# Loading one half of a weight tile in eight small transfers, one behind each of the next eight weight transfers

## The chip, the cores and the metric

The kernel runs on one core of a Trainium2 chip. The metric is device time in microseconds (us) of a whole execution; the profile gives the span of the same execution, which is some 1.7 us shorter. The kernel before takes 437.2 us; its trace comes from a slower execution, of 438.8 us (span 437.0).

## The reference, cut to what matters

```python
def reference(q, k, v, f, w_r, w_i, w_ch):         # names shortened
    # q, k, v: (8, 8, 576, 64); attention with a decay from f, causal
    x = attention(q, k, v, f)                      # ... (8, 576, 512)
    X = np.fft.rfft(x, axis=1)[:, :64]             # 64 modes
    Yr = einsum('bmd,mde->bme', Xr, w_r) - einsum('bmd,mde->bme', Xi, w_i)
    Yi = einsum('bmd,mde->bme', Xr, w_i) + einsum('bmd,mde->bme', Xi, w_r)
    y = np.fft.irfft(Y, n=576, axis=1)
    u = x + y
    return u + np.maximum(u @ w_ch, 0.0)
```

`w_r` and `w_i` have 64 x 512 x 512 fp32 elements each, 134 MB together. Reading them sets the pace: 163.73 MB are read from HBM in 437 us.

## The kernel before

The weights come in 64 tiles. Each tile has a `w_r` and a `w_i` transfer, issued by Pool (GpSimd), which also casts fp32 to bf16. A transfer reads 1 MiB. Tiles go through a ring of nine buffers; attention runs on TensorE meanwhile, and the matmuls of a tile (`emit_modes`) are put between attention steps.

```python
NRING = 9
wpool = ctx.enter_context(tc.tile_pool(name="wpool", bufs=NRING))
keep = tc.keep_in_program_order

def pool_dma(dst, src):
    keep(nc.gpsimd.dma_start(dst, src))

def emit_w_load(n):
    dc, g = tile_of(n)
    if n < NTH:                                  # the first 32 tiles
        wb = wb_tile(n, MG, 2 * D)
        for t, src in enumerate((moe_w_r, moe_w_i)):
            pool_dma(
                wb[t:128:2, :, :],               # 64 partitions
                src[g * MG : (g + 1) * MG, dc * 128 : (dc + 1) * 128, :]
                .rearrange("m (p r) e -> p m (r e)", r=2),
            )
    else:                                        # the last 32: 128 partitions each
        wb = wb_tile(n, 2, M2, 2 * D)
        ...
                pool_dma(wb[:, t, ms, :], src[...]...)
    wtiles[n] = wb

# ... in the attention loop, step s:
    if s > B:
        while nmode < (s - B) * NTH // (NS - B):
            emit_modes(nmode)                    # matmuls of one tile
            nmode += 1
            next_w()                             # load of the next one
```

The softmax here doesn't subtract the row's maximum and nothing guards it: scores larger than these inputs give would overflow.

## Time and profile before

| | before |
|---|---|
| time, median of 3 timed runs | 437.21 us (436.98 to 437.32) |
| span in the trace | 437.0 us |
| transfers from Pool until the last weights | 178, over 8 semaphores in turn |
| last weights landed | 400.66 us |
| start of the last eight weight matmuls | 401.18 us |
| spread of the 16 engines at that landing | 8.03 us |

### The profile page before, as it was taken

The numbers are of one execution on the slowest core, as the hardware profiler recorded it, in microseconds if no ns is written. First come the engines' busy times: TensorE is split into PE (matmuls) and PEld (weight loads), VectorE is DVE, ScalarE is ACT, GpSimd is POOL, SyncE is SP. The second block draws the span as 40 slices with busy tenths as digits, with TensorE's granted clock in tenths as the row PEclk, the third lists the DMA queues.
The fourth block names the chain that finished last, engine by engine and source line by source line (L and its number), as shares of the span: only waits on it lengthen the run. The fifth ranks groups of instructions, "written<-read, shape, count | busy, mean of one in ns | idle before, by whom it ended". The sixth has DMA issues, their size and how long they took to land.

```text
span 437.0 us, 12197 instructions
## 1 busy us (share of the span) xinstructions
PE 359.5 (82%) x5247; PEld 245.5 (56%) x5265; DVE 263.3 (60%) x658; ACT 224.6 (51%) x340; POOL 128.9 (29%) x202
## 2 busy tenths in 40 slices
PE   3787799998897887978778796999999688998880
PEld 2454666676666665656556664666665354554440
DVE  5797778877565655655657677333334353753891
ACT  2887478775534537446355473234335242742780
POOL 7333332233233233232332231323232223200600
PEclk9996699998866858556668688699999898998997
DMA  8999999999999999999999999999999999993797
GB/s 185 233 235 244 230 236 238 237 214 234 233 215 236 228 220 237 211 237 233 215 237 211 211 212 211 211 211 211 211 211 212 211 211 211 211 207 73 253 366 270
DMA packets 50981, 97.37 MB, mean 223 GB/s; under 512 B 3792, under 2 KB 12976, under 8 KB 50928
## 3 DMA queue, kind: packets, MB, share of 16 engines
q0 software_dynamic: 46688, 86.16, 100.6%
q1 hardware_dynamic: 3920, 9.91, 6.3%
q8 instruction: 41, 0.67, 0.6%
q10 hardware_dynamic: 320, 0.52, 0.5%
q14 instruction: 12, 0.10, 0.1%
HBM read 163.73 MB, written 9.44 MB: 396 GB/s over the span
## 4 chain that ended last, share of the span: by engine, by line
PE 31%; DMA 29%; ACT 12%; DVE 11%; issue 4%; ACTq 0%; DVEq 0%; POOL 0%
DMA wb<-in_moe_w_i_dram 27%; ACT E L574 8%; PE pav L612 7%; PE ps L567 6%; PE A L188 5%; PE tp L305 5%; DMA stv<-in_v_dram 3%; DVE QTs L320 2%; PE px L655 2%; PE vp L539 2%; ACT KT L318 2%; PE pz L826 2%; PE pu L826 1%; DVE os L1004 1%; DVE XT L669 1%
## 5 line engine op out<-in xcount | busy, mean ns | idle before, releaser
L574 ACT ACTIVATE E<-ps 128x1024 bf16<-128x1024 f32 (+1 forms) x128 | 101.5, 853 | 22.8 <-PE ps L567 12.7
L188 PE MATMUL A<-XT,wb 128*128 128x16 bf16 x1984 | 70.3, 181 | 14.6 <-DMA wb<-in_moe_w_i_dram 9.6
L188 PEld LDWEIGHTS <-wb 128*128 128x128 bf16 x1984 | 63.5, 99 | 28.6 <-issue 11.9
L93 POOL DMA_DIRECT2D wb<-in_moe_w_r_dram x64 | 42.5, 664 | 120.7 <-DMA wb<-in_moe_w_r_dram 24.5
L567 PE MATMUL ps<-QTs,KT 64*128 64x64 bf16 (+4 forms) x384 | 57.6, 320 | 18.2 <-ACT E L574 16.3
L93 POOL DMA_DIRECT2D wb<-in_moe_w_i_dram x64 | 42.4, 663 | 86.6 <-DMA wb<-in_moe_w_i_dram 42.9
L612 PE MATMUL pav<-va,E 128*128 128x65 bf16 (+1 forms) x1088 | 55.5, 210 | 3.1 <-DVE x_all L634 2.6
L612 PEld LDWEIGHTS <-E 128*128 128x128 bf16 (+1 forms) x1088 | 45.5, 115 | 17.5 <-issue 8.1
L589 DVE TENSOR_TENSOR E<-E,trimask 128x256 bf16<-128x256 bf16 (+2 forms) x128 | 36.9, 303 | 20.2 <-ACT E L574 20.0
L324 ACT COPY VT<-tp 128x640 bf16<-128x640 bf16 (+1 forms) x32 | 23.2, 762 | 33.5 <-PE tp L305 33.5
L865 ACT CAST XW<-pxw 128x512 bf16<-128x512 f32 x36 | 20.7, 586 | 35.8 <-PE pxw L858 23.5
L567 PEld LDWEIGHTS <-KT 64*128 64x128 bf16 x384 | 19.2, 99 | 32.8 <-issue 21.1
L908 ACT CAST XW<-pB 128x512 bf16<-128x512 f32 x36 | 20.9, 586 | 31.4 <-PE pB L826 25.8
L318 ACT COPY KT<-tp 128x640 bf16<-128x640 bf16 (+1 forms) x32 | 22.0, 751 | 26.2 <-PE tp L305 26.0
L907 DVE CAST x_all<-pA 128x512 bf16<-128x512 f32 x36 | 24.9, 692 | 16.7 <-PE pA L826 15.2
L858 PE MATMUL pxw<-wch,yy 128*128 128x512 bf16 x133 | 33.7, 386 | 1.2 <-issue 0.7
L320 DVE COPY QTs<-tp 128x640 bf16<-128x640 bf16 (+1 forms) x32 | 23.3, 767 | 14.2 <-PE tp L305 14.0
L634 DVE TENSOR_TENSOR x_all<-pav,rcp 128x384 bf16<-128x384 f32 x64 | 29.2, 456 | 0.9
L153 DVE TENSOR_TENSOR YTe<-A,Yacc 128x128 bf16<-128x128 f32 x16 | 5.9, 368 | 33.2 <-PE A L188 33.2
L623 DVE RECIPROCAL rcp<-pav 128x6 f32<-128x6 f32 x64 | 12.1, 190 | 22.6 <-PE pav L612 21.8
L826 PEld LDWEIGHTS <-ident_bf 64*64 64x64 bf16 (+1 forms) x300 | 14.5, 110 | 17.0 <-issue 9.6
L539 PE MATMUL vp<-ident_bf,VT 128*128 128x128 bf16 x160 | 17.2, 249 | 4.8 <-DVE QTs L320 4.3
(143 smaller groups left out, 609.8 us busy)
## 6 DMA issues: line engine op xcount, KB each, us to landing
wb<-in_moe_w_r_dram POOLq DMA_DIRECT2D x62, 512.0 KB, 17.2
wb<-in_moe_w_i_dram POOLq DMA_DIRECT2D x62, 512.0 KB, 17.8
stv<-in_v_dram POOLq DMA_DIRECT2D x10, 576.0 KB, 15.4
out_dram<-os SPq DMA_DIRECT2D x10, 512.0 KB, 6.3
stk<-in_k_dram POOLq DMA_DIRECT2D x11, 288.0 KB, 15.4
stq<-in_q_dram POOLq DMA_DIRECT2D x11, 288.0 KB, 15.2
wx<-in_v_dram POOLq DMA_DIRECT2D x5, 576.0 KB, 15.1
out_dram<-uo SPq DMA_DIRECT2D x3, 512.0 KB, 3.6
```

What stands on the lines that cost most here:

```text
L93: keep(nc.gpsimd.dma_start(dst, src))
L188: nc.tensor.matmul(A[:, eb, mi, :], lhsT=w_of(mi, eb * 128), rhs=x_of(m), start=(i == 0), stop=(i == len(terms) - 1),)
L318: nc.scalar.copy(rows(KTs[pr % 2][:, :, 0:S]), tv)
L320: ins = nc.vector.tensor_copy(rows(QT[pr][:, :, :]), tv)
L539: nc.tensor.transpose(vp[:, sc, :, :].rearrange("p b d -> p (b d)"), VTs[s // 2 % 2][:, h, sc * 128 : (sc + 1) * 128], ident_bf[:, :],)
L567: nc.tensor.matmul(ps[:, b, o : o + n], lhsT=KTs[pr % 2][bs, h, jb * 128 : (jb + 1) * 128], rhs=QT[pr][bs, h, jb * 128 + c0 : jb * 128 + c ...
L574: nc.scalar.activation(E[:, :, piece * 512 : piece * 512 + w], ps[:, :, 0:w], ACT.Exp, scale=scale,)
L589: nc.vector.tensor_tensor(dg, dg, tr, ALU.mult)
L612: nc.tensor.matmul(pav[64 * half : 64 * half + w, slot, :], lhsT=E[:, b, c : c + (w - 1) * st + 1 : st], rhs=va[:, jb, b, :], start=(n == ...
L634: nc.vector.tensor_tensor(xo, pi, ri, ALU.mult)
L826: return nc.tensor.matmul(p, lhsT=lhsT, rhs=rhs, start=first, stop=not first, skip_group_check=True)
L858: nc.tensor.matmul(pxw[:, :], lhsT=xT[:, eb, i * 128 : (i + 1) * 128], rhs=wch[:, eb, :], start=(eb == 0), stop=(eb == NDC - 1),)
```

## The change

It is meant to move work from one half of the 16 transfer engines to the other. The `w_r` part of tile 17 (index 16) is not loaded in one transfer on all engines, but in eight transfers of eight partitions, one behind each of the next eight weight transfers; a tiny transfer of eight partitions goes ahead of each, and only moves the place at which the next small one starts.

```diff
+    UPPER = 16
+    tiny = const.tile([8, 8, MG, 4], BF16, name="tiny")
+    eighths = []
+
-    def pool_dma(dst, src):
+    def pool_dma(dst, src, more=False):
         keep(nc.gpsimd.dma_start(dst, src))
+        for pair in eighths[:1] if more else ():
+            for d, s in pair:
+                keep(nc.gpsimd.dma_start(d, s))
+            eighths.pop(0)
...
             for t, src in enumerate((moe_w_r, moe_w_i)):
+                if n == UPPER and t == 0:
+                    for j in range(8):
+                        rows = src[
+                            g * MG : (g + 1) * MG, dc * 128 + 16 * j :, :
+                        ][:, 0:16, :].rearrange("m (p r) e -> p m (r e)", r=2)
+                        big = wb[16 * j : 16 * j + 15 : 2, :, :], rows
+                        small = tiny[:, j, :, :], rows[:, :, 0:4]
+                        eighths.append((small, big))
+                    continue
                 pool_dma(
...
+                    True,
                 )
```

More of the change, by code (lines that the diff above doesn't have):

```diff
@@ L132, in emit_modes @@
         wb = wtiles.pop(n)
+        assert n != UPPER or not eighths
         nm = MG if n < NTH else M2
```

## The prediction

> **What bounds the kernel now.** I read the page's slices first, then its queue part, then who waited for whom on the Pool engine, then the chain of waits, then the last part of the timeline.
>
> ```profile
> DMA  8999999999999999999999999999999999993797
> ...
> q0 software_dynamic: 46688, 86.16, 100.6%
> ...
> q8 instruction: 41, 0.67, 0.6%
> ...
> q14 instruction: 12, 0.10, 0.1%
> HBM read 163.73 MB, written 9.44 MB: 396 GB/s over the span
> ```
>
> The transfer engines are busy in every slice until the weights are in; nearly all of it is the Pool queue (q0). Two small queues fetch instructions: 41 blocks of 16,384 bytes on q8, and q14. They look like nothing (0.6% and 0.1%), but that is a mean over 16 engines.
>
> ```profile
> POOL wb L93 <- DMA wb<-in_moe_w_r_dram: 55.2, 31, 2.5
> POOL wb L93 <- DMA wb<-in_moe_w_i_dram: 55.2, 33, 2.7
> ```
>
> Pool itself spends its time waiting for earlier weight transfers: the built program gives its transfers eight semaphores in turn, so one is issued when the eighth before it has landed on all its engines. Eight are in flight.
>
> ```profile
> 276.12 18.28 DMA wb<-in_moe_w_i_dram
> 294.40 0.29 issue
> 294.69 19.60 DMA wb<-in_moe_w_i_dram
> 314.28 0.29 issue
> 314.57 19.60 DMA wb<-in_moe_w_i_dram
> ```
>
> From 276 to 395 us the chain is transfer after transfer, each issued 0.29 us after the landing that freed its semaphore.
>
> ```profile
> 393.50 0.21 PE L188 MATMUL A<-XT,wb 128*128 128x16 bf16 x2
> ...
> 395.07 0.91 PE L188 MATMUL A<-XT,wb 128*128 128x16 bf16 x30 [1.36 <-DMA wb<-in_moe_w_i_dram]
> ...
> 401.18 0.36 PE L172 MATMUL A<-XT,wb 128*128 128x16 bf16 x8
> ```
>
> TensorE waits 1.36 us for the weights of the last tile but one, and starts the last eight of the last tile at 401.18, 0.52 us after its last piece landed (400.66 in the trace). So the end of the kernel, some 36 us later, hangs on the *last* landing of the last weights, and could follow it forward by about 1.4 us before TensorE itself is the bound.
>
> **The view that the change is about** is not on the page. Each Pool transfer leaves 16 semaphore increments in the trace, one per transfer engine. In order of time, relative to the last of the 16, in us:
>
> ```
> landing at   7.5 us: -1.07 to -0.85 (nine), -0.64 to -0.45 (five), -0.35, 0
> landing at 395.0 us: -7.44 -7.40 -7.29 -7.22 -6.89 -6.67 -6.30 | -4.30 | -3.03 -2.95 -1.40 -1.21 -1.17 -0.76 -0.73 0
> ```
>
> A transfer has landed when the slowest engine is done, and that engine is 7.4 us behind the fastest when the last weights come. The increments carry no engine's name, so I followed each lane from transfer to transfer (a lane keeps its place to 0.1 us until it jumps). Eight lanes jump by about 1.2 us four or five times each, and end 7.27, 6.56, 6.45, 6.31, 6.18, 5.99, 4.43 and 4.37 us behind the three fastest. Eight never make that jump: seven end between -0.04 and 1.09, one creeps to 3.05 in steps of 0.4 to 0.6. The times of the q8 blocks (39 before 400 us) match the jumps, and the blocks' durations repeat with period eight (974, 974, 961, 892, 893, 949, 945, 936 ns): TensorE's instructions are fetched by eight of the sixteen engines in turn. The creeping lane fits q14's blocks of 322 ns.
>
> **What the Trainium skill says.**
> - "Runtime: NRT & Kernel Launch", section "Instruction fetch mechanics": instructions are refilled in 16 KiB blocks by the sequencer's own transfer queue. The trace agrees (41 of 16,384 bytes). The page calls the cost mostly hidden; here one block holds its engine back about 1.2 us.
> - "DMA: Bandwidth & Descriptors", "Why a DMA increments its semaphore by 16 and not by 1": from Pool all 16 engines post an increment whatever the shape; a transfer of k < 16 runs on k consecutive engines from a round-robin cursor. The kernel before shows the 16 increments; it has no transfer of fewer than 16 partitions from Pool, so the cursor is shown by nothing here.
> - The same page, "Specifications": about 27 GiB/s per engine. Here a weight transfer of 1 MiB read takes 2.485 us on an undisturbed lane: 65,536 bytes per engine, 26.4 GB/s. Agrees roughly; the engines run at their limit.
> - The same page, "Rules for kernel authors": below 64 KB a transfer is mostly overhead. The kernel before has none in its busy stage.
>
> **The change part by part.** It takes tile 17's w_r transfer away (64 partitions, all engines alike), and brings the same bytes in eight transfers of 8 partitions. With k = 8 each uses eight engines; the tiny one (8 partitions too) moves the cursor by eight first, so that all eight big ones fall on the same half and the tiny ones on the other. The intent must be to take work from the half that fetches instructions. In the built program the eighths stand behind the transfers of w_i of tile 17 to w_r of tile 21 (issued between 119 and 147 us now); TensorE needs tile 17 only nine tiles later.
>
> Per engine, a = cost of one extra transfer in the queue:
> - Half relieved: -2.485 us, plus 16 a, plus the tiny pieces (32 of 16 bytes per engine).
> - Half loaded: -2.485 + 8 x 16,384 bytes / 27.36 GB/s (the slope between 36,864 bytes in 1.437 and 65,536 in 2.485) = +2.31 us, plus 16 a.
> - a: that line leaves 1.437 - 1.347 = 0.09 us at zero bytes; yet w_ch has twice the descriptors of a weight transfer in 2.44 us, so it may be nearer 0. I take 0.05: 16 a = 0.8 us. Tiny pieces: 0.5 us (a guess).
>
> If the relieved half is the fetching one, its slowest lane goes from 7.27 to 7.27 - 2.485 + 0.8 + 0.5 = 6.1; the loaded half's slowest goes from 3.05 to 3.05 + 2.31 + 0.8 = 6.2. The last landing comes 7.27 - 6.2 = 1.1 us earlier. Of the 1.36 us that TensorE waits there, this fits: the end moves by 1.1 us. 437.2 - 1.1 = **436.1 us**.
>
> Beside other work: 15 more Pool issues of about 0.5 us (14 issues of 16 KB take some 0.5 us each now) while Pool idles most of the time. No compute is touched.
>
> **The rivals.**
> 1. *The big ones land on the fetching half, or on four of it.* For it: nothing in the trace names the half, and the cursor could start elsewhere. Against: the tiny transfers make no sense unless someone knew the half. Then 7.27 becomes 7.27 + 2.31 + 0.8 = 10.4: the end is 3.1 us later, 440.3 us. The same comes out if a transfer of 8 partitions always takes the same engines and these fetch.
> 2. *The ring of eight runs dry.* Tiny and small transfers take semaphores, so that when w_i of tile 19 is issued only two full transfers (4.95 us) lie ahead on the relieved half; less 0.3 for the wait and about 1.3 for two issues, 3.3 us. Against: at 82.0 us in the kernel before, an issue ended with 2.97 us ahead on the fastest lane and no gap followed. A gap would cost a few tenths at most, and mainly on the fast lanes, which have time.
> 3. *Nothing moves.* If a is 0.09, 16 a is 1.44 and the gain shrinks to 0.4 us; if the tiny pieces cost 0.2 us each on an engine, to about 0. That is 436.8 to 437.2 us. With a = 0.02 it is 1.6 us, and TensorE's 1.36 us of slack caps it: about 435.8.
>
> **Range and chances.** I give the intended half 0.72, with 435.4 to 437.2 us, middle 436.1; the wrong or mixed half 0.28, with 439 to 441. The middle of both together is a little over 436.1: **436.3 us**; 8 in 10 from **435.2** to **440.2**, wide on the slow side for rival 1. Two per cent is 8.7 us; no branch reaches it: faster 0.005, within 0.985, slower 0.01.
>
> **What would show it.** Right: before the last weights the spread of the 16 increments falls from 7.4 to about 5 to 6 us, with the two groups merged instead of seven and nine apart; TensorE's wait of 1.36 us before the last tile but one shrinks or moves earlier with the landing; the chain from 276 us stays transfer after transfer; the engines' share stays at 9 in every slice. From 165 to about 220 us the loaded half should lag, so landings come about 1 to 1.5 us *later* than before. Wrong: the spread grows to about 10 us (rival 1); Pool's transfers around 120 to 165 us are issued late with a dip in the transfer slices (rival 2); the spread falls as told but every lane is late by the same amount (rival 3).

## More of the kernel before

The order of Pool's transfers is pinned (`keep`); the order of the matmuls among the attention work is not: the scheduler chooses it when the kernel is built, from when it expects data.

The columns are 40 equal slices of the span (10.9 us each); PEclk is the granted TensorE clock in tenths, GB/s what the transfer engines moved:

```profile
PEclk9996699998866858556668688699999898998997
GB/s 185 233 235 244 230 236 238 237 214 234 233 215 236 228 220 237 211 237 233 215 237 211 211 212 211 211 211 211 211 211 212 211 211 211 211 207 73 253 366 270
```

The transfer engines move 207 GB/s or more in every slice after the first until the weights are in. The clock drops to half in the attention part and, for one slice or so, late.

## The result, and the profile after

The changed kernel takes 440.93 us (440.61 to 441.39, 4 runs) beside 437.23 us (436.98 to 437.32): ratio 1.0086, 95% interval 1.0069 to 1.0104. A ratio is the mean time of one kernel's runs over that of the other's of the same rounds, so not quite the ratio of the medians. The change makes the kernel 3.7 us slower; predicted were 436.3 us and a range up to 440.2. A second set on another chip gave 441.21 us and 1.0090. All outputs are right.

The page of the changed kernel (slices of 11.0 us):

```profile
DMA  8999999999999999999999999999999999994797
GB/s 181 234 235 244 232 235 238 236 218 230 235 211 231 197 203 224 220 238 226 222 235 212 211 210 212 210 211 212 211 212 210 212 210 211 211 211 88 251 362 271
...
q0 software_dynamic: 47696, 86.16, 100.5%
...
q8 instruction: 41, 0.67, 0.6%
```

The digits of the DMA row hide it, the GB/s row shows it: in the 14th and 15th slice, 143 to 165 us, the engines moved 197 and 203 GB/s, where they moved 228 and 220 before. That is where the small transfers are. The bytes are the same; q0 has 1008 packets more.

Who Pool waited for, in us, times, longest:

```profile
POOL wb L97 <- DMA wb<-in_moe_w_i_dram: 44.6, 28, 2.2
POOL wb L97 <- DMA wb<-in_moe_w_r_dram: 33.1, 18, 2.3
POOL wb L97 <- PE A L207: 32.8, 10, 7.7
```

The waits for earlier transfers fell from 110.4 to 77.7 us, and the wait for TensorE's weight matmuls is 32.8 us, where the first trace before has

```profile
POOL wb L93 <- PE A L188: 13.2, 5, 5.7
```

This sum shows nothing by itself: in the second trace of the kernel before (below) it is 30.9 us, with a longest of 7.7 us. What is new is one place, the issue of `w_r` of tile 26, nine tiles behind tile 17. Before and after:

```profile
180.09 0.63 POOL L93 DMA_DIRECT2D wb<-in_moe_w_r_dram  x1 [1.71 <-PE tp L305]
188.70 0.63 POOL L97 DMA_DIRECT2D wb<-in_moe_w_r_dram  x1 [7.04 <-PE A L207]
```

The semaphore of this transfer had been free for 0.5 us in both traces of the kernel before, and for 5.8 us here. There TensorE frees a ring buffer later than before, which the prediction excluded.

The chain of waits is as before, transfer after transfer with 0.29 us between:

```profile
289.09 18.14 DMA wb<-in_moe_w_i_dram
307.23 0.29 issue
307.52 19.59 DMA wb<-in_moe_w_i_dram
327.12 0.29 issue
327.41 20.28 DMA wb<-in_moe_w_i_dram
```

TensorE at the end:

```profile
398.01 0.91 PE L207 MATMUL A<-XT,wb 128*128 128x16 bf16 x30 [0.92 <-DMA wb<-in_moe_w_i_dram]
...
403.43 0.36 PE L191 MATMUL A<-XT,wb 128*128 128x16 bf16 x8 [0.39 <-DMA wb<-in_moe_w_i_dram]
```

The last eight matmuls start at 403.43 us, 2.25 us later than before, again behind the last landing (403.39). The end follows the landing: 439.5 - 403.39 = 36.1 us, before 437.0 - 400.66 = 36.3 us.

Now the 16 increments, which no view prints; they are taken from the trace's semaphore records. The first fence has their times relative to the last at the landing of the last weights, the second the step of the lanes from the tiny transfer to the eighth behind it. A lane is one of the 16 engines as the increments show it, without a name. A step is the difference of the n-th landings, the earliest first; where one lane overtakes another, the two mix.

```
last weights, before         -8.03 -8.03 -7.90 -7.85 -7.51 -7.30 -6.35 -4.74 -3.21 -3.11 -1.53 -1.23 -1.19 -1.07 -0.90 0
last weights, after          -7.07 -7.04 -6.84 -6.60 -6.56 -6.53 -6.16 -5.43 -4.13 -3.39 -0.92 -0.77 -0.75 -0.33 -0.25 0
last weights, after (second) -5.64 -5.61 -5.50 -5.42 -5.29 -5.03 -4.75 -4.25 -2.53 -2.48 -1.83 -1.43 -0.18 -0.16 -0.13 0
```

```
after,          1st eighth (135.6 us)  0.20 0.46 0.19 0.19 0.22 0.28 0.35 0.20 | 0.20 0.21 0.56 0.55 0.54 0.50 0.67 0.73
after (second), 8th eighth (165.5 us)  0.18 0.18 0.18 0.19 0.18 0.20 0.20 0.20 | 0.48 0.42 0.72 0.72 0.56 0.63 0.64 0.74
```

A lane that carries an eighth takes 0.42 to 0.75 us, one that does not 0.18 to 0.2; the values between them are such mixtures. The eighths went to the **late** lanes, those that also fetch TensorE's instructions. This is the prediction's first rival.

### The profile page after: what moved, and what is told of

The parts are those of the page before. It is cut to its first block, busy times and chain, and to the rows that moved or that the text cites. A ratio compares the mean times of both kernels' runs of the same rounds, so it can differ in the third digit from the quotient of the medians.

```text
span 439.5 us, 12212 instructions
## 1 busy us (share of the span) xinstructions
PE 359.4 (82%) x5247; PEld 245.8 (56%) x5265; DVE 263.8 (60%) x658; ACT 225.0 (51%) x340; POOL 137.4 (31%) x217
## 4 chain that ended last, share of the span: by engine, by line
PE 36%; DMA 26%; DVE 11%; ACT 10%; issue 4%; POOL 1%; ACTq 0%; DVEq 0%
DMA wb<-in_moe_w_i_dram 25%; PE pav L631 8%; ACT E L593 7%; PE A L207 6%; PE ps L586 6%; PE tp L324 6%; PE px L674 2%; PE vp L558 2%; DVE QTs L339 2%; ACT KT L337 2%; DVE os L1023 1%; DVE XT L688 1%; DVE E L608 1%; PE px L699 1%; PE pz L845 1%
## 5 line engine op out<-in xcount | busy, mean ns | idle before, releaser
L97 POOL DMA_DIRECT2D wb<-in_moe_w_r_dram x63 | 42.3, 672 | 124.5 <-PE A L207 32.8
L586 PE MATMUL ps<-QTs,KT 64*128 64x64 bf16 (+4 forms) x384 | 58.5, 327 | 17.6 <-ACT E L593 15.6
L97 POOL DMA_DIRECT2D wb<-in_moe_w_i_dram x64 | 42.5, 663 | 67.6 <-DMA wb<-in_moe_w_i_dram 36.1
L642 DVE RECIPROCAL rcp<-pav 128x6 f32<-128x6 f32 x64 | 12.1, 190 | 23.1 <-PE pav L631 22.4
```

Of the source, the lines that this page charges most:

```text
L586: nc.tensor.matmul(ps[:, b, o : o + n], lhsT=KTs[pr % 2][bs, h, jb * 128 : (jb + 1) * 128], rhs=QT[pr][bs, h, jb * 128 + c0 : jb * 128 + c ...
```

## The experiments

There were eighteen runs, three of them repeats, each on one chip with the kernel before beside it. "Mean" and "slowest" below are how much longer the lanes took than in the kernel before from the landing of `w_i` of tile 16 to that of `w_i` of tile 22 (the window of the small transfers), the mean over the 16 lanes and the last lane. "The ring" is from here on that of the eight semaphores, and it is "dry" when a lane has too little work left in it to stay busy.

### Tiny one behind

```diff
-                        eighths.append((small, big))
+                        eighths.append((big, small))
```

> Each tiny transfer stands behind its eighth instead of ahead of it; bytes, counts and places in the queue are the same, so if a cursor deals out halves, tiny and big ones change halves. Theory A (eighths fell on the fetching half, and every one of the 16 small transfers costs about 0.18 us on all 16 engines): the fetching lanes get -2.485 + 16 x 0.18 = +0.4 us, the other half carries the data, the end is at about 437.6 us (437.0 to 438.4). Theory B (the half plays no part, only the number of small transfers and the ring of eight): as the changed kernel, 440.5 to 441.3 us.

> The changed kernel with the tiny transfer behind (as in the first experiment) once more, on another chip: if the half explains part of the 3.7 us, it is faster than the changed kernel beside it by 1 to 3 us; last weights landing 2 to 3 us earlier than there. If the half explains nothing, within 0.5 us of it.

Measured: 440.02 us (438.14 to 442.81), ratio 1.0069 (1.0036 to 1.0101), and on the other chip 440.61 us, 1.0076 (1.0061 to 1.0092), where the changed kernel beside it took 441.21. The steps of the lanes turned round: in the first trace the first eighth took 0.61 to 0.74 us on lanes among the nine earliest and 0.16 to 0.17 on the latest.

```
tiny behind, 1st eighth (134.5 us)  0.33 0.41 0.28 0.61 0.62 0.63 0.73 0.65 0.74 | 0.16 0.17 0.37 0.45 0.19 0.17 0.17
tiny behind, 8th eighth (164.8 us)  0.17 0.17 0.16 0.18 0.17 0.16 0.18 0.20 | 0.64 0.65 0.67 0.62 0.63 0.66 0.66 0.68
```

So the order of the pair decides the half, and the prediction's intended half needs the tiny one *behind*. But by the eighth eighth the loaded lanes are themselves the latest eight. In the first trace the last weights landed at 400.34 us, 3.1 us before the changed kernel's, and the profiled span was 436.4 us; TensorE waited as before:

```profile
395.20 0.91 PE L207 MATMUL A<-XT,wb 128*128 128x16 bf16 x30 [0.98 <-DMA wb<-in_moe_w_i_dram]
...
400.39 0.36 PE L191 MATMUL A<-XT,wb 128*128 128x16 bf16 x8 [0.19 <-DMA wb<-in_moe_w_i_dram]
```

In the second trace they landed at 403.30, as late as the changed kernel's. (The first trace is of the fastest of that kernel's six executions, 438.14 us.) One trace of this kernel is therefore not enough to tell its landing; the times are. They say: right half 2.8 to 3.3 us slower than the kernel before, and only some 0.6 us faster than the wrong half on the same chip. Both theories of the first expectation missed the 440.02 us. The second asked for 1 to 3 us and a landing 2 to 3 us earlier, and missed both. Something common to both orders costs more than the half does.

### No tiny one

```diff
-                        eighths.append((small, big))
+                        eighths.append((big,))
```

> The eight eighths without the tiny ones: eight small transfers instead of sixteen, and halves that alternate. Theory A: -2.485 + 8 x 0.18 + 4 eighths of about 0.4 us data = +0.5 us on every lane, about 437.8 us. Theory B (only the count): half of the loss, about 439 us. Theory C (only the wrong half, small transfers free): -2.485 + 4 x 0.6 = 0, 437.2 us.

Measured: 439.43 us, ratio 1.0045 (1.0021 to 1.0069). Eighths now fall on the two halves in turn. The time is that of theory B; the lanes don't bear it out: mean +0.24 us, last weights at 400.48 us, as before. The profiled span is 439.1 us nevertheless, 38.6 us after the landing instead of 36. The granted clock tells why; the window is 396 to 406 us, the columns are length, then busy us of PE, PEld, DVE, ACT and POOL with their numbers of instructions, then granted clock, DMA share, GB/s. Without tiny ones:

```profile
396.00:406.00 10.00, 9.77 (x84) 3.90 (x84) 3.32 (x8) 1.78 (x4) 0.51 (x1) 0.54 0.24 48
```

and the second trace of the kernel before (below):

```profile
396.00:406.00 10.00, 9.10 (x115) 4.41 (x113) 5.82 (x10) 4.60 (x7) 3.07 (x7) 1.00 0.31 76
```

At a clock of 0.54 TensorE needs 9.77 us for 84 matmuls, where at 1.00 it does 115 in 9.10 us (not all of the same shapes). In every trace the clock drops once or more between 340 and 412 us, for some 3 to 10 us at half; a drop before the last weights is hidden behind their landing, one after lengthens the end. In the eighteen experiments and the two first traces the end came 34.6 to 37.0 us after the landing where the clock from 396 to 406 us was 0.83 or more (37.4 in one), and 36.8 to 38.6 us where it was 0.52 to 0.73. This is the noise of some 1 to 2 us in single executions.

### Small transfers without a shift of bytes

`w_r` of tile 17 stays one transfer; behind each of the next eight weight transfers come two tiny ones, of 8 partitions (16 in the second kernel).

```diff
-                        big = wb[16 * j : 16 * j + 15 : 2, :, :], rows
-                        small = tiny[:, j, :, :], rows[:, :, 0:4]
-                        eighths.append((small, big))
-                    continue
+                        small2 = tiny[:, 8 + j, :, :], rows[:, :, 2:4]
+                        small = tiny[:, j, :, :], rows[:, :, 0:2]
+                        eighths.append((small, small2))
```

> w_r of tile 17 whole as in the kernel before; in the same places eight pairs of tiny transfers of 8 partitions whose data nobody reads: the cost of 16 small transfers alone, no load moved. Theory A: 16 x 0.18 = +2.9 us, about 440.1 us, every lane late by the same. Theory C (small transfers cost as predicted, 0.05 us and a little): 437.5 to 438.2 us.

> As the tiny pairs, with 16 partitions each, so that all 16 engines take part. If a small transfer costs 0.18 us whatever its shape: about 440.1 us as with 8 partitions. If the cost comes with using fewer than 16 engines (the trace has 48 four-byte packets for each 8-partition transfer, 16 for a full one): a third to a half, 438 to 438.7 us.

Measured: 438.71 us, 1.0038 (1.0013 to 1.0064), and 439.13 us, 1.0041 (1.0019 to 1.0062): the two agree, so the number of partitions of a tiny transfer plays no part that could be seen. Both are slower than the kernel before although hardly any byte was added, and both times lie between the theories. TensorE's order is nearly the old one here (the matmuls of two tiles moved, by 24 others each), and Pool issues `w_r` of tile 26 0.5 us after its semaphore.

The lanes show how. Each tiny transfer lands 0.18 us after the one ahead of it, but the full transfer behind the pair then takes 2.2 us instead of 2.48: two tiny ones and a full one take 2 x 0.18 + 2.2 = 2.56 us, so each costs some 0.04 us, which is the prediction's a = 0.05. Sixteen of them make 0.7 us. The mean is +2.30 and +1.85 us, and it is uneven: +3.27 and +2.96 on the four earliest lanes, +1.63 and +1.32 on the four latest. The rest is idle time of engines that have run out of work. In this window of the kernel before some 13 us of work lie ahead on the slowest lane when a transfer is issued, and 9 to 10 on the fastest; here it falls to 4 to 6 and to about 1 us. Much of the loss falls on one transfer: the `w_i` transfer whose issue ended at 145.34 us, with 1.59 us ahead on the fastest lane and 3.91 us on the slowest, took 0.65 to 1.43 us more than 2.2 on every lane (1.1 us in the mean; 0.5 us in the second kernel). So a lane idles before its queue is quite empty; why even the one with 3.91 us ahead did is not shown. Pool's own issues, 0.55 us for each small transfer, also delay some of the following ones past their semaphore; that part was not separated.

### The order on TensorE alone

The built programs differ on TensorE: the changed kernel has the 192 matmuls of six tiles in one lump. Four of the tiles, 128 matmuls, were moved there, tile 17 by two attention steps. The timelines of TensorE, only weight matmuls; before:

```profile
166.52 1.13 PE L188 MATMUL A<-XT,wb 128*128 128x16 bf16 x32
...
183.97 1.14 PE L188 MATMUL A<-XT,wb 128*128 128x16 bf16 x32
```

after:

```profile
187.36 1.03 PE L207 MATMUL A<-XT,wb 128*128 128x16 bf16 x32
188.91 1.17 PE L207 MATMUL A<-XT,wb 128*128 128x16 bf16 x32 [0.52 <-DVE Yacc L218]
```

The next kernel loads `w_r` of tile 17 whole, eight weight transfers later. Its order on TensorE is, instruction for instruction, that of the changed kernel; it has no small transfer.

```diff
-                    for j in range(8):
-                        ...
-                        eighths.append((small, big))
+                    for j in range(7):
+                        eighths.append(())
+                    rows = src[g * MG : (g + 1) * MG, dc * 128 : (dc + 1) * 128, :]
+                    eighths.append(
+                        ((wb[0:128:2, :, :], rows.rearrange("m (p r) e -> p m (r e)", r=2)),)
+                    )
```

> The w_r part of tile 17 whole, as in the kernel before, but eight weight transfers later: no small transfer, every lane the same bytes, and in the built program exactly the TensorE order of the changed kernel (the 192 matmuls of tiles 17 to 22 in one clump). Theory 'the new TensorE order costs time' (it frees the ring slots late): 438.5 to 440 us, and w_r of tile 26 is issued some 6 us after its semaphore is free. Theory 'only the lanes count': 437.2 us within 0.5, whatever Pool waits for. Lanes before the last weights spread 7 to 8 us in both.

Measured: 438.2 us (436.89 to 439.95), ratio 1.0021 (1.0000 to 1.0042). The wait is there, longer than expected (its semaphore had been free for 10.4 us):

```profile
177.40 0.73 POOL L96 DMA_DIRECT2D wx<-in_v_dram  x1 [1.78 <-DVE va L562]
189.71 0.63 POOL L96 DMA_DIRECT2D wb<-in_moe_w_r_dram  x1 [11.58 <-PE A L205]
```

Mean in the window -0.01, at the end +0.9 us, the last landing 0.4 us earlier than in the first trace before. Both theories named ranges that the 0.9 us fall between. The new order costs 0 to 1.8 us by the interval, well below the 3.7.

### The kernel before once more

> The kernel before once more, for a second trace of it and for the spread between equal kernels: 437.2 us within 0.4, ratio 1.000 within 0.002, last weights landing within 1 us of 400.66, spread of the lanes 7 to 8 us, issue of w_r of tile 26 within 1 us of its semaphore.

Measured: 437.72 us, ratio 1.0011 (0.9991 to 1.0030). The last weights landed at 399.55 us, just outside the 1 us that was expected, and the lanes' mean was 396.33 us (396.29 in the first trace): the mean repeats to 0.1 us, the last lane only to 1 us. The changed kernel's second run repeats this too:

> The changed kernel once more, for a second trace: 440.9 us within 0.6, last weights landing within 1 us of 403.4, w_r of tile 26 issued 5 to 7 us after its semaphore is free.

Measured: 441.21 us, 1.0090 (1.0075 to 1.0105), landing 402.75 us. `w_r` of tile 26 waited 9.6 us, not 5 to 7. The dip is there again (214 and 200 GB/s in the 14th and 15th slice; 225 and 223 in the second trace before). Slowest lane in the window +3.03 us in the first trace and +3.04 in the second; the prediction's sum for the wrong half is +3.1.

### The same shift early

Tile 2 (index) in place of tile 17, whose buffer is free from the start; tiny behind, and tiny ahead.

```diff
-    UPPER = 16
+    UPPER = 2
-                        eighths.append((small, big))
+                        eighths.append((big, small))     # first kernel only
```

> The eighths of tile 2 in place of tile 17, tiny one behind each, so that the big ones fall on the half that fetches nothing, early, where no ring slot has to come free and without the clump on TensorE. Theory 'the half decides, by the sum of the prediction': lanes before the last weights spread 5 to 6 us instead of 7.4, landing 1.1 us earlier, 436.1 us (435.6 to 436.6). Theory 'sixteen small transfers cost on all lanes': 437.5 us or more. If the ring runs dry here too, the gain shrinks: 436.6 to 437.2.

> As the run before with the tiny one ahead of each, so that the big ones fall on the half that fetches, as in the changed kernel, but early and without the clump. Theory 'the half decides': landing 3.1 us later than in the kernel before, spread about 10 us (no dry ring on the fast lanes), 440.2 us (439.5 to 440.8). Theory 'the clump or the dry ring made the changed kernel slow': 437.0 to 438 us.

Measured: 442.3 us, 1.0122 (1.0095 to 1.0150), and 442.61 us, 1.0150 (1.0114 to 1.0187). Both expectations missed for the right half and for the wrong one. A new stall hit both: the scheduler again moved matmuls, and in the first kernel a `w_r` transfer was issued at 87.14 us, 12.1 us after its semaphore was free, where the kernel before waits 8.1 us at 81.4 us. By then 2.1 us of work was left on the slowest lane and none on the fastest. The lanes came out of it nearly level, so their mean at the end is +4.8 and +4.4 us. This place does not isolate the half.

### The same shift late

Of two late tiles (indices 50 and 56) half of `w_r` is loaded ahead of time, in eight pieces of 8 partitions (8,192 bytes per engine) behind the eight weight transfers of the four tiles before. No byte arrives later than before.

```diff
+    def start_early(n):                          # called at the load of tile n - 4
...
+        early[n] = wb = wb_tile(n, 2, M2, 2 * D)
+        for j in range(8):
+            rows = moe_w_r[g * M2 : (g + 1) * M2, D // 2 + 16 * j :, :][
+                :, 0:16, :].rearrange("m (p r) e -> p m (r e)", r=2)
+            big = wb[8 * j : 8 * j + 8, 0, :, :], rows
+            small = tiny[:, 8 * UPPER.index(n) + j, :, :], rows[:, :, 0:4]
+            eighths.append((big, small))         # second kernel: (small, big)
...
-                        wb[:, t, ms, :],
+                        wb[p0:, t, ms, :],       # p0 = 64 for w_r of these tiles
```

> The same shift of bytes between the halves as in the changed kernel, but late, where no ring slot is short and no attention loads stand between: of tiles 50 and 56 half of w_r each in eight pieces of 8 partitions (8,192 bytes per engine), one behind each of the eight weight transfers before that tile, a tiny one behind each piece. Nothing arrives later than before for TensorE, the order of its instructions is as before up to there. Theory 'the half decides, by the sum of the prediction': fetching half -2.48 + 0.8, other half +2.31 + 0.8, slowest lane 1.1 us earlier, the spread of the lanes before the last weights falls to 5 to 6 us; 436.1 us (435.7 to 436.6). Theory 'small transfers cost on all lanes': 437.5 us or more.

> As the run before, tiny one ahead of each piece: the pieces fall on the half that fetches. Theory 'the half decides': slowest lane 3.1 us later, spread about 10 us, 440.3 us (439.6 to 441). Difference to the run before 4.2 us, with the same transfers, the same TensorE order and the same waits; theory 'the ring of eight or TensorE's order did it': no difference above 0.7 us.

Measured: 442.01 us, 1.0112 (1.0092 to 1.0132), and 443.93 us, 1.0139 (1.0111 to 1.0166). The second is slower by 1.2 us (ratios) to 1.9 us (medians), where the half's sum says 4.2; both lie far above their numbers, the first in the range of the rival theory (437.5 or more). The second's trace is of its fastest execution, 440.47 us. The lanes relative to the last at the last weights:

```
late, right half  -1.85 -1.65 -1.65 -1.61 -1.56 -1.50 -1.42 -1.38 -1.25 -1.23 -1.21 -0.97 -0.48 -0.31 -0.01 0
late, wrong half  -1.90 -1.83 -1.82 -1.75 -1.75 -1.57 -1.22 -1.21 -1.07 -0.55 -0.46 -0.45 -0.41 -0.40 -0.39 0
```

The spread did not fall to 5 us or grow to 10: it is 1.9 us in both. In the first, the spread fell from 5.1 to 1.3 us within four weight transfers (`w_i` number 46 to 48, counted from 0), the earliest lanes losing about 5 us and the latest about 1. One weight transfer, one piece and one tiny one take three of the eight semaphores, so the ring holds fewer than three full transfers: at 312 us 0.02 us of work was left on the fastest lane when an issue ended. Pool waits for the *slowest* lane before each issue; an early lane can then be ahead of it by no more than the ring holds. The early lanes lost the lead that the shift was to spend, and the bytes shifted onto them came on top.

One thing was not held fixed, here and in the next four kernels, against the expectation: from tile 45 or 46 on, the scheduler put TensorE's weight matmuls behind up to 48 to 105 other matmuls. In all six, Pool issued one transfer at 355 to 361 us 2.3 to 2.9 us after its semaphore was free, which the kernel before does not do after 294 us. What this is worth in the late kernels was not measured.

### Late, pairs further apart

Four late tiles (indices 48, 52, 56, 60) with two pieces each, one pair behind every third to fifth weight transfer; tiny behind, tiny ahead. Then three pieces each behind every second to fourth. Then the dense late kernel without tiny ones.

```diff
-        for pair in eighths[:1] if more else ():
+        turn[0] += bool(more and eighths)
+        for pair in eighths[:1] if more and turn[0] % 3 == 0 else ():   # third kernel: % 2
```

> Late tiles 48, 52, 56 and 60: two pieces of 8 partitions of each, a tiny one behind each piece, one pair behind about every fourth weight transfer (8 pairs in 32). Theory 'dry ring': here five of eight semaphores hold full transfers, no lane runs dry, the early lanes keep their lead, and the half's sum comes out: fetching half -1.24 + 0.4 = -0.84 us, other half +1.16 + 0.4; landing 0.8 us earlier, 436.4 us (436.0 to 437.0), spread 6 to 7 us. Theory 'each small transfer costs on all lanes' (the 4.7 us of the dense late kernel over 32 small transfers, so 16 cost 2.4): 439 us or more.

> The same with the tiny one ahead, so that the pieces fall on the half that fetches. Theory 'dry ring' with the half's sum: slowest lane +1.16 + 0.4 = +1.56 us, 438.8 us (438.2 to 439.4), 2.4 us above the run before. Theory 'each small transfer costs': 440.5 us or more. Theory 'the half does not matter': equal to the run before within 0.5.

> As the first of these with three pieces per tile, one pair behind every second to fourth transfer (12 pairs). If the ring stays full: fetching half -1.86 + 0.6 = -1.26 us, 436.0 us. If it runs short on the early lanes (about four full transfers in flight, where there were eight): spread 3 to 5 us, 436.5 to 438 us. If each small transfer costs: 440 us.

> The late dense kernel (tiles 50 and 56, sixteen pieces, one behind each transfer) without the tiny ones: pieces fall on the two halves in turn, so no bytes are shifted, and a full transfer takes two semaphores instead of three. Theory 'dry ring': about 10 us ahead at issue in place of 16, early lanes partly held back, the last landing +0.4 us, 437.3 to 438.3 us. Theory 'each small transfer costs' (16 of them): 439.5 us or more.

| kernel | time, us | ratio | last weights | spread | mean at the end |
|---|---|---|---|---|---|
| 8 spaced, right half | 440.62 | 1.0073 (1.0052 to 1.0093) | 400.37 | 4.6 | +1.5 |
| 8 spaced, wrong half | 441.81 | 1.0096 (1.0078 to 1.0114) | 401.96 | 5.7 | +2.2 |
| 12 spaced, right half | 440.10 | 1.0059 (1.0040 to 1.0079) | 401.39 | 5.3 | +2.7 |
| dense, no tiny | 440.65 | 1.0071 (1.0053 to 1.0089) | 401.03 | 4.2 | +2.3 |

All four lie above the numbers of the dry ring, and in the range that its rival gave, a price for each small transfer (439 or more, 440.5 or more, 440, 439.5 or more). The right half is again faster than the wrong one, by 1.0 to 1.2 us, with landings 1.6 us apart (2.4 expected). The ring was not full: in the first of them, after four of the eight pairs, the work ahead on the fastest lane still fell to 1.3 to 2.1 us. Twelve pairs cost no more time than eight, which speaks against a price per small transfer; the lanes' mean, +2.7 instead of +1.5 us, speaks for one. At this place the question stays open. What I can't explain in full is the time of the first: its trace, of its fastest execution, has the last landing between those of the two traces before, and ends 37.3 us after it, with a clock of 0.54 from 396 to 406 us. In all four traces the one half-clock stretch between 340 and 412 us began at 395 us or later (mean clock from 396 to 406 us 0.52 to 0.73), while in the two of the kernel before it was partly or wholly earlier (0.83 and 1.00). That fits the added time, but whether the timed executions all had it is not shown.

### Half as many pairs

At the place of the changed kernel, tile 17: the upper 64 rows whole, the lower ones in four eighths, tiny one behind; a pair behind each of the next four weight transfers, or behind every second.

```diff
-                    for j in range(8):
+                    for j in range(4):
...
-                        eighths.append((small, big))
-                    continue
+                        eighths.append((big, small))
+                p0 = 64 if n == UPPER and t == 0 else 0
...
+        for pair in eighths[:1] if more and turn[0] % 2 == 1 else ():   # second kernel
```

> Tile 17: the upper 64 rows of w_r in one transfer as before, the lower ones in four eighths, one behind each of the next four weight transfers, a tiny one behind each (right half). Half's sum alone: fetching half -1.24 + 0.4 = -0.84, other half +1.16 + 0.4; mean of the lanes +0.36 us. Theory 'dry ring': in the window of four the mean of the lanes grows by 0.8 to 1.4 us instead (half of what eight pairs took), and the last landing is no earlier than before; 437.3 to 439 us.

> The same four eighths and tiny ones, a pair behind every second weight transfer. Theory 'dry ring': four or more full transfers stay in the ring, the mean of the lanes grows by 0.2 to 0.5 us in the window, as the half's sum says (+0.36), and the last landing comes 0.4 to 0.9 us earlier than in the dense one. Theory 'each small transfer costs': the mean grows as in the dense one, within 0.2 us. Time 436.4 to 437.5 us, with up to 0.9 us more for TensorE's changed order.

Measured: 437.8 us, 1.0006 (0.9985 to 1.0027), and 438.62 us, 1.0012 (0.9993 to 1.0032): both as fast as the kernel before within the interval. Mean in the window +0.44 and +0.23 us; the sum says +0.36. The dense one ran dry only with its fourth pair, and on the earliest lanes alone: the full transfer behind it took 4.24 and 3.72 us on the first two instead of 2.2. The dry ring's number for it, 0.8 to 1.4 us, was too high; and 0.21 us between the two is too little to tell them apart as I had meant to. The spaced one missed its own numbers: its last weights landed at 400.93 us, later than the dense one's, and its time lies just above the range. TensorE's order differs too: four tiles moved in it as in the changed kernel, two in the dense one. But together with the kernels of sixteen small transfers they settle the question for tile 17: eight small transfers cost 0.2 to 0.4 us of lane time, sixteen in the same window 1.3 to 3.0 us. A price per transfer would double; what grows here out of proportion is the idle time of the engines when too little work is left ahead of them. That came with the fourth pair here, and with the second of the tiny pairs.

The dense one's last weights landed at 399.59 us, and the lanes at the end agree with the half's sum (late lanes -0.3 to -1.1 us, early lanes +1.3 to +2.2). TensorE:

```profile
393.80 0.91 PE L210 MATMUL A<-XT,wb 128*128 128x16 bf16 x30 [1.46 <-DMA wb<-in_moe_w_i_dram]
...
400.40 0.36 PE L194 MATMUL A<-XT,wb 128*128 128x16 bf16 x8
```

The wait on the last weights is gone in this trace. No kernel of this study beats the kernel before: this one equals it.

### The experiments at tile 17 side by side

| kernel | small transfers | shift to | mean, window: sum / measured | slowest: measured | ratio |
|---|---|---|---|---|---|
| after | 16 | late lanes | +0.7 / +3.05, +2.19 | +3.03, +3.04 | 1.0086, 1.0090 |
| tiny behind | 16 | early lanes | +0.7 / +1.27, +2.13 | +1.90, +2.74 | 1.0069, 1.0076 |
| tiny pairs | 16 | none | +0.8 / +2.30, +1.85 | +1.85, +1.85 | 1.0038, 1.0041 |
| no tiny | 8 | none | +0.4 / +0.24 | +0.53 | 1.0045 |
| four eighths, dense | 8 | early lanes, half | +0.36 / +0.44 | +1.07 | 1.0006 |
| four eighths, spaced | 8 | early lanes, half | +0.36 / +0.23 | +1.41 | 1.0012 |
| whole, later | 0 | none | 0 / -0.01 | 0.00 | 1.0021 |

The sum of a row is the mean of the prediction's two halves: (-1.7 + 3.1) / 2 = 0.7, or 0.05 us per transfer where no bytes move.

## Why the prediction was wrong, point by point

The half decided only which branch of the prediction came true. The step that failed for both branches is point 2: with the half that was intended the kernel still took 440.02 and 440.61 us instead of 436.1.

1. **The half (failed).** The step was "I give the intended half 0.72", on the argument that "the tiny transfers make no sense unless someone knew the half". The eighths fell on the fetching half: the steps of the lanes show it in two traces, and reversing the pair moves them. The prediction's own first rival, 440.3 us with +3.1 us on the slowest lane, came out in its total: +3.03 and +3.04 us on the slowest lane, 440.93 us. That it fits so well is partly luck: its sum has 0.8 us for sixteen small transfers, which alone cost the slowest lane 1.85 us (tiny pairs). The intent of a change is no evidence of what it does; only a trace could have named the half, and the kernel before has no transfer of fewer than 16 partitions from Pool.
2. **The dry ring (failed: mechanism named, size wrong).** "A gap would cost a few tenths at most, and mainly on the fast lanes, which have time." The prediction reckoned 3.3 us ahead, on the relieved half, at the issue of `w_i` of tile 19. There the slowest lane had 5.0 to 5.5 us ahead, in two traces of each order of the pair, but the fastest only 0.7 to 1.3: Pool waits for the slowest lane, so a lane that leads it by 4 to 5 us has that much less ahead. The dip in the slices that was to show this rival is there (197 and 203 GB/s). In dense kernels it took 0.6 to 2.4 us of the lanes' mean beyond the sum, and 1.0 us on the slowest lane even of the tiny pairs (1.85 less 0.8). Nor do the fast lanes "have time" in the right-half case: their lead is what the shift was to spend. For this reason the prediction's favoured branch, 436.1 us, would have failed with the right half too: 440.0 and 440.6 us.
3. **The spread.** "The spread grows to about 10 us (rival 1)" did not come: 7.07 and 5.64 us. In the window the ring held the four earliest lanes back by 2.2 to 3.3 us more than before while the last one took 3.0 us more, so most lanes are late by nearly the same amount. That is also the sign named for rival 3, with another cause.
4. **"No compute is touched" (failed).** The scheduler moved 128 matmuls, and `w_r` of tile 26 was issued 5.8 and 9.6 us after its semaphore was free, instead of 0.5. Alone this costs 0.9 us, with an interval from 0 to 1.8. The order could have been read from the built program beforehand.
5. **The cost of a small transfer (right).** a = 0.05 us: 0.04 measured. The separate guess of 0.5 us for the eight tiny ones was not needed. (A slip without effect: the 27 GiB/s that the prediction cites are 29.0 GB/s, so the measured 26.4 are 9% less.)
6. **TensorE follows the landing (right).** The end comes 36.1 us after it, before 36.3, unless a half-clock stretch falls behind it.

How the 3.7 us divide can't be read to better than about 1 us. With ratios that were measured apart: order of TensorE 0.9 us, sixteen small transfers without shift 1.7 (438.71 and 439.13 less the 437.25 beside them), the half the remaining 1.1. In the four pairs of kernels that differ only in the half and ran on the same chip, the right one is faster by 0.23 to 0.28 per cent in three (early, late, spaced) and by 0.14 at tile 17, by the difference of their ratios: 0.6 to 1.2 us. That fits, but the intervals are some 0.9 us each way, and the parts need not simply add. In the early pair, whose place does not isolate the half, the medians are only 0.3 us apart. By the landing alone the change costs 2.97 us (means of two traces each: 400.1 to 403.07).

## What to carry to other kernels

Count in semaphores as well as in bytes: a small transfer takes the same place in the issue ring as a large one, so a row of them drains the queue, and the engines that were ahead fall back towards the slowest. To shift work between transfer engines, learn from a trace which engines are behind and where a short transfer starts, keep the short ones to a few, and look at the order of all engines in the built program, since an arrival that moves changes what the scheduler does elsewhere. Compare single traces only beside a second trace of the same kernel: here the last landing of equal kernels differed by up to 3 us (on two chips).

## What the Trainium skill lacked or had wrong

- "DMA: Bandwidth & Descriptors", "Why a DMA increments its semaphore by 16 and not by 1": it says that a transfer of k < 16 from Pool takes k consecutive engines from a round-robin cursor. The trace agrees: with 8 partitions eight lanes take 0.42 to 0.75 us and eight 0.18, and a tiny transfer ahead or behind exchanges them; whether the eight are neighbours, nameless lanes don't show. It does not say where the cursor stands when a kernel starts. Here the first eight-partition transfer fell on the lanes that fetch no TensorE instructions in all four traces that were looked at (two with the tiny one first, two with the eighth first).
- "Runtime: NRT & Kernel Launch", "Instruction fetch mechanics": it calls a block's cost mostly hidden and does not say which transfer engines fetch. Here blocks of 16,384 bytes set back one lane by about 1.2 us each, eight of the 16 lanes in turn (39 blocks before 400 us), and the last of these is 7 to 8 us late at the last weights.
- "DMA: Bandwidth & Descriptors", "Rules for kernel authors": below 64 KB one pays mostly overhead. In a full queue a tiny transfer costs a lane 0.04 us; the price comes from the places in the ring (sixteen in a row: 1.9 to 2.3 us of mean lane time).
- No page that I read says that with eight transfers in flight an early engine can't stay further ahead of the slowest than the ring holds (spread pressed from 5.1 to 1.3 us in four weight transfers).
- "TensorE: Matmul & The Clock Gate", "What's actually happening": activity is said to release the throttle. Here TensorE was busy for 9.77 of the 10 us from 396 to 406 us and had a granted clock of 0.54; drops of some 3 to 10 us to half come late in every trace, at a time that differs between executions.
